# First norm of chunk 0 moved into the convolution, turned blocks given to engines by name, one weight load on another queue, and three changed orders in the main loop

## The chip, the cores and the metric

One core of a Trainium2 chip runs one launch of one program. The core has five engines that run their own instruction streams in order and meet at semaphores: TensorE (PE, matrix products; PEld is its weight load), VectorE (DVE), ScalarE (ACT), GpSimd (POOL) and SyncE (SP). The last two, and ACT now and then, also issue DMA transfers. The metric is the time of one execution on the device in microseconds (us). Lower is better.

## What is computed

Two kinds of layer alternate, and the kernel computes the output and, through the derivative of the whole, the gradients of eight inputs:

```python
def _A_ref(q, k, v, shift_k, ssm_k, ssm_D):
    k_shift = sum over 4 taps of k shifted in time * shift_k
    kv = k_shift * v
    y = irfft(rfft(kv, 2S) * rfft(ssm_k, 2S))[:S]      # a long convolution
    return q * (y + kv * ssm_D)

def _B_ref(x, w1, w2):
    return silu(x @ w1) @ w2

x = A_q
x = x + _A_ref(_layernorm(x), A_k, A_v, A_shift_k, A_ssm_k, A_ssm_D)
x = x + _B_ref(_layernorm(x), B_w1, B_w2)
x = x + _A_ref(_layernorm(x), ...)       # the same weights again
x = x + _B_ref(_layernorm(x), ...)
```

The sequence has S = 2048 places, the model D = 448 channels, the hidden layer F = 1792; all arrays are bf16. The convolution y does not depend on x, so it is computed once and used by both A layers. The results are x and the gradients by q, k, v, shift_k, ssm_k, ssm_D, w1 and w2.

## The kernel before

The work has three stages. `_ssm_prefix` (0 to about 103 us) computes the convolution with Fourier matrices on PE. `Main.run` (about 103 to 512 us) takes the sequence in four chunks of 512 places (four tiles of 128) through both layers, forward and back. `_ssm_suffix` and `Jobs` (to the end) carry the gradient through the convolution and sum the gradients of w1 and w2.

**Order.** The order of PE's instructions in the main stage is the order in which the program records them. A scheduler orders the other engines, mostly by the order of recording as operands become ready, and each engine then keeps its list in order: an instruction that waits holds up all that stand behind it. Tiles of one tag share a fixed number of buffers, and an allocation waits until the buffer's last user is done. A POOL transfer waits, besides its operands, until the eighth POOL transfer before it has landed.

**The prefix around the change.** Two passes over the channel halves h = 0, 1 each run four rounds. A round makes the four-tap convolution of four tiles (`conv`, PE L392), copies it (ACT `ks`, L395), stores it (POOL, L397), multiplies it by v (DVE L398), and does the first Fourier step of the round before (`stage1_kv`, PE L408, copies to A1kv). In the pass h = 0 a round also turns two blocks of the filter's transform (`turn`, PE L370, 16 transposes of 128x128 a block, one copy of 128x2048). In the pass h = 1 a round also does the second Fourier step of the filter (PE L217, copies to ZK). The first layer norm of chunk 0 (`ln0`, a generator over `_ln_steps`) takes one step in each round of h = 1: the statistics of one tile (DVE L271, L274). Behind the rounds it runs to its end: `ln_ve` (DVE L277), the power -1/2 on POOL (L279, `rstd`), `ln_nmr` (DVE L282), four `na` (ACT L285) and a store of them (POOL L290). Then come the half swaps: 14 transfers on POOL (L253, L254) that write the filter's spectrum with real and imaginary halves exchanged, and which must land before the products can use them; four stores of the spectrum (L445); w1, loaded by three transfers on SP (L447 to L449) and in part cleared by POOL (L450). Then seven blocks of A1kv are turned (L370 again), with copies given to ACT or DVE by a running estimate of both loads (`bal.pick`). After that come 14 chunks: a Fourier step (PE L217), a copy (ACT or DVE, again `bal.pick`), the product with the spectrum and its swapped copy (`pab`, DVE L471), 16 small matmuls (`ps_v`, PE L235, L236) two chunks later, and a copy of those (ACT).

**The main loop around the change.** `H` makes the hidden layer (PE L513 into `ps_h`; ACT takes Silu to `aT`, L673, and copies the input of Silu to `dT`, L678; a few copies are DVE's, L676). `O` multiplies by w2 (PE L695 into `ps_o`; DVE adds the result to X, L699, which frees one of two PSUM buffers of the tag "po"). `G` and `N` are the way back: N multiplies by w1 transposed (PE L741 into `ps_n`, the same two buffers; ACT copies it, L745, and DVE runs a chain of small operations for each tile, L915 to L920, L748 to L755). `T` transposes a normed chunk (PE L580, ACT copy L581). `fwd0b(c)` is the second norm of chunk c: statistics (L271, L274), `ln_ve` (L277), POOL's power (L279), four `n` (L287). `fwd0(c)` is the first norm and the gate (L287, L621, L622). `weave` takes a pattern of letters, one step of a generator for each letter. One step of O or N is half a tile, seven matmuls of 128x448; two steps of N are a tile. One step of H is one pair of hidden blocks, seven in a chunk. In iteration c the order is O of chunk c in layer 2, the product of ghT with dT (DVE L866), N with H of chunk c+1 in layer 1, O, then G, and N with H of chunk c+1 in layer 2.

Of the kernel before, what the change touches and what calls it, by code (L numbers as in the profile page):

```python
# [17 lines left out]
P = 128  # L18
# [90 lines left out]
def _copy(nc, eng, out, in_):  # L109
    if eng is nc.scalar:  # L110
        return nc.scalar.copy(out, in_)
    return eng.tensor_copy(out, in_)
# [148 lines left out]
def _ln_steps(k, pool, c, src, si, n_g, groups=((0, 4),), pin=False, eng=None, behind=None, store=()):  # L261
    nc = k.nc
    for lo, hi in groups:
        n = hi - lo
        st = pool.tile([P, 4, 6], FP32, name="ln_st", tag="ln_st", bufs=1)
        mv = pool.tile([P, 4, 2], FP32, name="ln_mv", tag="ln_mv", bufs=2)
        for tl in range(lo, hi):
            with ExitStack() as es:
                if behind:
                    es.enter_context(k.tc.issue_after(behind[tl].ins))  # L270
                i = nc.vector.bn_stats(out=st[:, tl, :], in_=src(tl))  # L271
            if pin:
                k.tc.keep_in_program_order(i)
            nc.vector.bn_aggr(out=mv[:, tl, :], in_=st[:, tl, :])  # L274
            yield
        ve = pool.tile([P, 4], FP32, name="ln_ve", tag="ln_ve", bufs=2)
        nc.vector.tensor_scalar(out=ve[:, 0:n], in0=mv[:, lo:hi, 1], scalar1=EPS, scalar2=None, op0=ALU.add)  # L277
        r = k.rstd[si][:, 4 * c:4 * c + 4]
        k.ln_pow = nc.gpsimd.tensor_tensor(out=r[:, lo:hi], in0=ve[:, 0:n], in1=k.mhalf[:, 0:n], op=ALU.pow)  # L279
        if eng is nc.scalar:  # L280
            nmr = pool.tile([P, 4], FP32, name="ln_nmr", tag="ln_nmr", bufs=1)
            nc.vector.scalar_tensor_tensor(out=nmr[:, lo:hi], in0=mv[:, lo:hi, 0], scalar=-1.0, in1=r[:, lo:hi], op0=ALU.mult, op1=ALU.mult)  # L282
        for tl in range(lo, hi):
            if eng is nc.scalar:
                nc.scalar.activation(n_g[:, tl, :], src(tl), ACT.Identity, bias=nmr[:, tl:tl + 1], scale=r[:, tl:tl + 1])  # L285
            else:
                k.ln_last = nc.vector.tensor_scalar(out=n_g[:, tl, :], in0=src(tl), scalar1=mv[:, tl, 0:1], scalar2=r[:, tl:tl + 1], op0=ALU.subtract, op1=ALU.mult)  # L287
    if si != 2 and store is not None:
        lo, hi = store or (groups[0][0], groups[-1][1])
        nc.gpsimd.dma_start(out=_pm(k.N_d[si][:])[:, 4 * c + lo:4 * c + hi, :], in_=n_g[:, lo:hi, :])  # L290
# [7 lines left out]
def _ssm_prefix(k):  # L298
    nc, tc = k.nc, k.tc
    bal = k.bal  # L300
    k_pm = _pm(k.A_k[0])
    v_pm = _pm(k.A_v[0])
    with ExitStack() as es:
# [20 lines left out]
        Zkv = A1K[:].rearrange("p a c n s -> p a (c n s)")  # L324
# [24 lines left out]
        for dc in range(ND):  # L349
            kview = ksb[dc].rearrange("p (n1 n2) -> p n2 n1", n2=16)  # L350
            pt = psum.tile([P, 2, 1024], BF16, name="ps_kt", **a_)
# [12 lines left out]
        bal.reset()  # L364
        A1Kf = A1K[:].rearrange("p a c n s -> p (a c n s)").rearrange("p (a b) -> p a b", b=P)

        def turn(src, dst, g):
            pt = psum.tile([P, 16, P], BF16, name="ps_tr", **a_)
            for i in range(16):
                nc.tensor.transpose(pt[:, i, :], src[:, 16 * g + i, :], k.ident[:])  # L370
            _copy(nc, bal.pick(2048, dve_ns=0.53), dst[:, 16 * g:16 * g + 16, :], pt[:])

        for jq in range(4):
            pt = psum.tile([DC, ND, 4, P], BF16, name="ps_kT", **a_)
# [47 lines left out]
        ln0 = _ln_steps(k, work, 0, lambda tl: k.x0c0[:, tl, :], 0, k.na0, pin=True, eng=nc.scalar)  # L422

        prev = None
        for h in range(2):
            for i, jq in enumerate((1, 2, 3, 0)):
                kvt = conv(h, jq)
                if prev:
                    stage1_kv(*prev)
                prev = (h, jq, kvt)  # L430
                if h == 0:
                    for g in (2 * i, 2 * i + 1):
                        if g < 7:
                            turn(A1Kf, Z, g)
                else:
                    _fft_stage2(k, Z, psum, cons_ka, range((0, 4, 8, 11)[i], (4, 8, 11, 14)[i]))
                    next(ln0, None)
        for _ in ln0:
            pass
        for i in range(7):  # L440
            _swap_halves_dma(k, KB, Ka, 2048 * i, 2048 * (i + 1), nc.gpsimd)
        stage1_kv(*prev)
# [1 line left out]
        for i in range(7):  # L444
            nc.gpsimd.dma_start(out=k.SPEC_d["K"][:, 2048 * i:2048 * (i + 1)], in_=Ka[:, 2048 * i:2048 * (i + 1)])  # L445
        k.w1sb = k.wk.tile([P, ND, F], BF16, name="w1sb", tag="WB")
        nc.sync.dma_start(out=k.w1sb[:, 0:3, :], in_=k.B_w1[0:384].rearrange("(c p) f -> p c f", p=P))  # L447
        nc.sync.dma_start(out=k.w1sb[64:128, 3, :], in_=k.B_w1[384:448, :])
        nc.sync.dma_start(out=k.w1sb[0:64, 3, 2 * P:], in_=k.B_w1[320:384, 2 * P:])  # L449
        nc.gpsimd.memset(k.w1sb[0:64, 3, 0:2 * P], 0.0)  # L450


# [2 lines left out]

        A1f = A1kv[:].rearrange("p a c n s -> p a (c n s)")
        for g in range(7):
            turn(A1f, Zkv, g)
        hold = []

        def cons_prod(ci, ps):
# [76 lines left out]
class Main:  # L538
# [245 lines left out]
    def run(self, es):  # L784
# [5 lines left out]
        def weave(pattern, **gens):  # L790
            for ch in pattern:
                next(gens[ch], None)
            for g in gens.values():
                if g is not jg:
                    for _ in g:
                        pass
# [6 lines left out]
        r = []  # L803
# [28 lines left out]
        r = []  # L832
# [4 lines left out]
        for c in range(4):  # L837

            aT2, dT2 = r
            self.slope(dT2)  # L840
            if c < 3:
                self.fwd0(c + 1)
            nT = self.nT() if c < 3 else None
            o = self.O(c, 1, aT2)
            steps("OOOO", O=o)
            if c in (1, 2):
                self.fwd0b(c + 1)
            if c == 0:
                weave("O" * 4, O=o)
                self.fwd0b(1)  # L850
            else:
                if c == 1:
                    gh2, g = gh21, g21
                else:
                    gh2 = []
                    g = self.G(gT, gh2)
                if c == 1:
                    weave("OGGOGGOTOT", O=o, G=g, T=self.T(self.n0[c + 1][1], nT))
                elif c < 3:
                    weave("OGOGGOGGGGTOT", O=o, G=g, T=self.T(self.n0[c + 1][1], nT))  # L860
                else:
                    jobs.start()
                    weave("OGOGGOGGGGO", O=o, G=g)
            for lo, hi in ((0, 4), (4, 7), (7, 8), (8, 12), (12, 13), (13, 14)):
                g = gh2[lo // 7][:, lo % 7:lo % 7 + hi - lo, :]
                nc.vector.tensor_tensor(out=g, in0=self.dpart(dT2, lo, hi), in1=g, op=ALU.mult)  # L866
            if c < 3:
                for hh in range(2):
                    self.store(("g", 1), gh2[hh], c, hh)
            gbc = gb  # L870
            n = self.N(c, 1, gh2, lambda tl: gbc[:, tl, :], self.n1[1], self.n1[0])
            G2 = self.X[:, 4 * c:4 * c + 4, :]
            gT = self.nT()
            gh1, dT0 = [], dT1
            tg = self.T(G2, gT)
            if c < 3:
                r = []
                if c == 0:
                    weave("NTNTNHNNHHNNHHNHH", N=n, T=self.T(self.n0[1][1], nT), H=self.H(c + 1, 0, nT, r, (10, 11)))
                else:  # L880
                    weave("NHNNHHNNHHNNHHN", N=n, H=self.H(c + 1, 0, nT, r))
                gb = gb_load(c + 1)
                aT, dT1 = r
                weave("OOOOOOTOTO", O=self.O(c + 1, 0, aT), T=tg)
                self.fwd1(c + 1, [self.chain] * 4)
                g = self.G(gT, gh1, dT0)
                if c:
                    gT = self.nT()
                    self.load_gT(c + 1, gT)
                    weave("G" * 7, G=g)  # L890
                else:
                    weave("G" * 7, G=g)
                self.slope(dT1, self.last_copy)
            else:
                weave("NJNJNJNJNJNJNJN", N=n, J=jg)
                for hh in range(2):
                    self.store(("g", 1), gh2[hh], c, hh)
                weave("J" * 11 + "TJJTJJJJ", T=tg, J=jg)
                weave("GGGJJGGJJGGJJ", G=self.G(gT, gh1, dT0, (1, 3, 5)), J=jg)
            for hh in range(2):  # L900
                self.store(("g", 0), gh1[hh], c, hh)
            n = self.N(c, 0, gh1, lambda tl: self.X[:, 4 * c + tl, :], self.n0[c][1], self.n0[c][0])
            if c < 3:
                r = []
                nT = self.nT()
                weave("NNTNTNHNNHHNNHHHH", N=n, T=self.T(self.n1[1], nT), H=self.H(c + 1, 1, nT, r, (10, 11)))
            else:
                weave("NJNNJNNJNNJN", N=n, J=jg)
        jobs.pool = None
# [473 lines left out]
```

## Time and profile before

| what | us |
|---|---|
| median of three runs | 716.89 (713.9 to 718.23) |
| the profiled execution | 716.31 |
| its span in the trace | 714.5 |
| PE busy in the span | 689.3 |
| DVE busy | 486.2 |
| ACT busy | 444.2 |
| POOL busy | 123.3 |

The span runs from the first to the last instruction in the trace; the time has 1.8 us more. A timeline row says when an instruction or a run of equal ones starts, how long it took, which engine, line and operation it is, the tiles (written <- read), their shapes, how many, and in brackets the idle time of that engine just before and what ended it. A row of waits gives the total, the number of times and the longest. Matmuls overlap, so a busy PE is a PE with work in its pipeline.

### The profile page before, as it was taken

The page shows a single profiled execution, that of the slowest core. Times are in us where ns is not written, and L with a number is a line of the kernel's source. Part 1 is how long each engine was busy: PE and PEld are TensorE (multiplying, and loading weights), DVE is VectorE, ACT ScalarE, POOL GpSimd, SP SyncE. Part 2 cuts the span into 40 slices and gives each one's busy share as a digit, 9 for nine tenths or more (in the row PEclk, how much of TensorE's full clock was granted, in tenths as well). Part 3 has the DMA queues.
Part 4 walks back from the last instruction along what each step waited for, and adds up shares of the span by engine and source line. Part 5 has one row for each costly group of instructions (what it writes and reads, how often), then busy time and mean ns, then how long its engine had stood idle before and what let it go on. Part 6 is the DMA issues. An engine that isn't in the chain of part 4 may idle for free.

```text
span 714.5 us, 12786 instructions
## 1 busy us (share of the span) xinstructions
PE 689.3 (96%) x5008; PEld 380.9 (53%) x5008; DVE 486.2 (68%) x1106; ACT 444.2 (62%) x582; POOL 123.3 (17%) x208
## 2 busy tenths in 40 slices
PE   6997899999999999999999999999999999999998
PEld 4886654434444444444444444544566666656655
DVE  4788776758887747877279723934258769869790
ACT  3878877686777868778677685132755555545200
POOL 1034420111011100111001100001212223353130
PEclk9999899999999999999999999999999999999999
DMA  9949998659969999499975999089999897879962
GB/s 303 305 146 234 342 287 255 168 139 270 236 146 235 215 240 242 116 243 231 224 179 133 233 229 365 3 187 249 309 413 357 291 343 245 266 274 377 354 181 95
DMA packets 196237, 172.59 MB, mean 242 GB/s; under 512 B 143090, under 2 KB 174194, under 8 KB 195024
## 3 DMA queue, kind: packets, MB, share of 16 engines
q1 hardware_dynamic: 181280, 115.30, 61.3%
q0 software_dynamic: 13344, 52.54, 20.9%
q10 hardware_dynamic: 1552, 3.94, 1.5%
q8 instruction: 39, 0.64, 0.4%
q14 instruction: 22, 0.18, 0.1%
HBM read 73.25 MB, written 60.10 MB: 187 GB/s over the span
## 4 chain that ended last, share of the span: by engine, by line
PE 62%; issue 8%; DVE 5%; ACT 4%; DMA 3%; POOL 2%; POOLq 0%; DVEq 0%; ACTq 0%
PE ps_d L995 12%; PE ps_n L741 12%; PE ps_h L513 11%; PE ps_g L513 10%; PE ps_o L695 7%; PE ps_d L1030 3%; ACT dT L688 2%; DMA ksf<-KS_d 1%; PE ps_t L580 1%; PE ps_gK L1305 1%; PE ps_tr L1211 1%; POOL rstd L279 1%; PE ps_d L1065 1%; PE ps_s L206 1%; DVE n L287 1%
## 5 line engine op out<-in xcount | busy, mean ns | idle before, releaser
L995 PEld LDWEIGHTS <-dstat 128*128 128x128 bf16 x768 | 72.5, 98 | 61.1
L513 PE MATMUL ps_h<-nT,w1sb 128*128 128x512 bf16 (+1 forms) x448 | 97.4, 380 | 2.6 <-ACT dT L678 1.9
L741 PE MATMUL ps_n<-w1T,ghT 128*128 128x448 bf16 x448 | 92.5, 353 | 0.8 <-DVE ghT L866 0.8
L695 PE MATMUL ps_o<-w2sb,aT 128*128 128x448 bf16 x448 | 88.5, 352 | 0.0
L513 PE MATMUL ps_g<-nT,w2T 128*128 128x512 bf16 (+1 forms) x392 | 82.9, 380 | 0.1
L723 ACT CAST ghT<-ps_g 128x512 bf16<-128x512 f32 (+1 forms) x74 | 54.1, 760 | 41.5 <-PE ps_g L513 41.2
L673 ACT ACTIVATE aT<-ps_h 128x512 bf16<-128x512 f32 (+1 forms) x82 | 60.0, 759 | 29.2 <-PE ps_h L513 27.6
L513 PEld LDWEIGHTS <-w1sb 128*128 128x128 bf16 (+1 forms) x448 | 35.5, 97 | 59.7 <-issue 25.4
L741 PEld LDWEIGHTS <-ghT 128*128 128x128 bf16 x448 | 43.2, 98 | 42.3 <-DVE ghT L866 1.7
L695 PEld LDWEIGHTS <-aT 128*128 128x128 bf16 x448 | 43.5, 98 | 40.1
L513 PEld LDWEIGHTS <-w2T 128*128 128x128 bf16 (+1 forms) x448 | 35.4, 97 | 55.1 <-issue 20.8
L915 DVE SCALAR_TENSOR_TENSOR lb_v<-lb_u,n 128x448 bf16<-128x448 bf16 x48 | 30.0, 624 | 46.8 <-ACT lb_u L745 46.3
L279 POOL TENSOR_TENSOR rstd<-ln_ve,mhalf 128x2 f32<-128x2 f32 (+2 forms) x27 | 23.0, 851 | 198.8 <-DVE ln_ve L277 198.8
L688 ACT ACTIVATE dT<-dT 128x1024 bf16<-128x1024 bf16 (+1 forms) x64 | 55.0, 940 | 0.1
L995 PE MATMUL ps_d<-n1m,dstat 128*128 128x448 bf16 x224 | 48.6, 352 | 0.0
L995 PE MATMUL ps_d<-n3m,dstat 128*128 128x448 bf16 x224 | 48.6, 352 | 0.0
L678 ACT CAST dT<-ps_h 128x1024 bf16<-128x1024 f32 (+1 forms) x50 | 42.8, 872 | 0.0
L745 ACT ACTIVATE lb_u<-ps_n,rstd 128x448 bf16<-128x448 f32 x32 | 20.7, 647 | 34.5 <-PE ps_n L741 26.3
L995 PE MATMUL ps_d<-X,dstat 128*128 128x448 bf16 x160 | 34.2, 353 | 0.0
L995 PE MATMUL ps_d<-go,dstat 128*128 128x448 bf16 x160 | 33.7, 353 | 0.0
L581 ACT COPY nT<-ps_t 128x1024 bf16<-128x1024 bf16 x20 | 20.2, 1008 | 18.7 <-PE ps_t L580 18.7
L866 DVE TENSOR_TENSOR ghT<-dT,ghT 128x512 bf16<-128x512 bf16 (+2 forms) x24 | 18.1, 778 | 19.2 <-ACT ghT L723 17.0
(217 smaller groups left out, 1245.1 us busy)
## 6 DMA issues: line engine op xcount, KB each, us to landing
dstat<-g_d SPq DMA_DIRECT2D x28, 512.0 KB, 5.6
dstat<-a_d SPq DMA_DIRECT2D x23, 512.0 KB, 7.1
a_d<-turned SPq DMA_DIRECT2D x16, 512.0 KB, 4.1
g_d<-turned SPq DMA_DIRECT2D x16, 512.0 KB, 3.9
a_d<-turned SPq DMA_DIRECT2D x16, 384.0 KB, 3.3
g_d<-turned SPq DMA_DIRECT2D x16, 384.0 KB, 3.3
N_d<-n POOLq DMA_DIRECT2D x10, 448.0 KB, 4.6
spec_K<-ZK POOLq DMA_DIRECT2D x7, 512.0 KB, 7.7
```

Source lines behind the costliest of these rows:

```text
L279: k.ln_pow = nc.gpsimd.tensor_tensor(out=r[:, lo:hi], in0=ve[:, 0:n], in1=k.mhalf[:, 0:n], op=ALU.pow)
L513: nc.tensor.matmul(ps(u, u + 1)[:, 0, :], lhsT=wT[h, b, ft * P:(ft + 1) * P], rhs=rhs[h, b, :], start=start, stop=stop)
L673: self.last_silu = nc.scalar.activation(aT[hh][:, o:o + hi - lo, :], ps(lo, hi), ACT.Silu)
L678: nc.scalar.copy(self.dpart(dT, 2 * fp + lo, 2 * fp + hi), ps(lo, hi))
L688: self.nc.scalar.activation(d[:, o:o + n, :], d[:, o:o + n, :], ACT.Derivative_silu)
L695: nc.tensor.matmul(po[:, :D], lhsT=aT[ft // 7][:, ft % 7, tl * P:(tl + 1) * P], rhs=self.w2sb[:, ft, :], start=(ft == 0), stop=(ft == NF - 1))
L723: nc.scalar.copy(g, ps(lo, hi))
L741: nc.tensor.matmul(pn[:, :D], lhsT=gh[ft // 7][:, ft % 7, tl * P:(tl + 1) * P], rhs=self.w1T[:, ft, :], start=(ft == 0), stop=(ft == NF - 1))
L745: nc.scalar.activation(u0[:], pn[:, :D], ACT.Identity, scale=k.rstd[2 * L + 1][:, t:t + 1], accum_out=cp[:, tl, 0:1])
L915: nc.vector.scalar_tensor_tensor(out=v[:], in0=u0, scalar=-1.0 / D, in1=n_t, op0=ALU.mult, op1=ALU.mult, accum_out=cp[:, 1:2])
L995: self.nc.tensor.matmul(ps[:, :D], lhsT=st[:, t, :], rhs=mov[:, t, :], start=(first and t == 0), stop=(last and t == NT - 1))
L1030: nc.tensor.matmul(ps[ft][:, :D], lhsT=get(t), rhs=mov[:, t, :], start=ft not in seen, stop=(last[ft] == i and t == hi - 1))
```

## The change

- `_ln_steps` yields once more, between POOL's power and what uses it. `ln0` takes its four steps of statistics in the rounds of h = 0 and its last two in the first two rounds of h = 1; the loop that ran it out is gone.
- The turned blocks of A1kv are copied by ACT (blocks 0, 3 and 6) and by DVE (1, 2, 4 and 5) by name, and the estimate of loads is reset behind them.
- w1 is loaded by POOL, behind the half swaps and the four stores, instead of SP.
- In iteration 0 the second norm of chunk 1 (`fwd0b(1)`) is recorded behind the product of ghT with dT instead of ahead of it.
- Iteration 0: the weave of N, T and H goes from NTNTNHNNHHNNHHNHH to NNTNTNHNNHHNNHHHH.
- Iterations 0, 1 and 2: the weave of N, T and H of layer 2 goes from NNTNTNHNNHHNNHHHH to NNTNTNHNHNHHNHHNH.

```diff
@@ _ln_steps
         k.ln_pow = nc.gpsimd.tensor_tensor(out=r[:, lo:hi], in0=ve[:, 0:n], in1=k.mhalf[:, 0:n], op=ALU.pow)
+        yield
         if eng is nc.scalar:
@@ _ssm_prefix
-        def turn(src, dst, g):
+        def turn(src, dst, g, eng=None):
...
-            _copy(nc, bal.pick(2048, dve_ns=0.53), dst[:, 16 * g:16 * g + 16, :], pt[:])
+            _copy(nc, eng or bal.pick(2048, dve_ns=0.53), dst[:, 16 * g:16 * g + 16, :], pt[:])
...
                         if g < 7:
                             turn(A1Kf, Z, g)
+                    next(ln0)
                 else:
                     _fft_stage2(k, Z, psum, cons_ka, range((0, 4, 8, 11)[i], (4, 8, 11, 14)[i]))
                     next(ln0, None)
-        for _ in ln0:
-            pass
...
-        nc.sync.dma_start(out=k.w1sb[:, 0:3, :], in_=k.B_w1[0:384].rearrange("(c p) f -> p c f", p=P))
-        nc.sync.dma_start(out=k.w1sb[64:128, 3, :], in_=k.B_w1[384:448, :])
-        nc.sync.dma_start(out=k.w1sb[0:64, 3, 2 * P:], in_=k.B_w1[320:384, 2 * P:])
+        nc.gpsimd.dma_start(out=k.w1sb[:, 0:3, :], in_=k.B_w1[0:384].rearrange("(c p) f -> p c f", p=P))
+        nc.gpsimd.dma_start(out=k.w1sb[64:128, 3, :], in_=k.B_w1[384:448, :])
+        nc.gpsimd.dma_start(out=k.w1sb[0:64, 3, 2 * P:], in_=k.B_w1[320:384, 2 * P:])
...
         for g in range(7):
-            turn(A1f, Zkv, g)
+            turn(A1f, Zkv, g, nc.vector if g % 3 else nc.scalar)
+        bal.reset()
@@ Main.run
             if c == 0:
                 weave("O" * 4, O=o)
-                self.fwd0b(1)
             else:
...
                 nc.vector.tensor_tensor(out=g, in0=self.dpart(dT2, lo, hi), in1=g, op=ALU.mult)
+            if c == 0:
+                self.fwd0b(1)
...
                 if c == 0:
-                    weave("NTNTNHNNHHNNHHNHH", N=n, T=self.T(self.n0[1][1], nT), H=self.H(c + 1, 0, nT, r, (10, 11)))
+                    weave("NNTNTNHNNHHNNHHHH", N=n, T=self.T(self.n0[1][1], nT), H=self.H(c + 1, 0, nT, r, (10, 11)))
...
-                weave("NNTNTNHNNHHNNHHHH", N=n, T=self.T(self.n1[1], nT), H=self.H(c + 1, 1, nT, r, (10, 11)))
+                weave("NNTNTNHNHNHHNHHNH", N=n, T=self.T(self.n1[1], nT), H=self.H(c + 1, 1, nT, r, (10, 11)))
```

## The prediction

> **What bounds the kernel now.** I read the page's busy times first, then PE's waits, then timelines of the three places that the diff touches.
>
> ```profile
> PE 689.3 (96%) x5008; PEld 380.9 (53%) x5008; DVE 486.2 (68%) x1106; ACT 444.2 (62%) x582; POOL 123.3 (17%) x208
> ...
> PE ps_v L235 <- DVE pab L471: 7.4, 5, 3.6
> ...
> PE ps_h L513 <- ACT dT L678: 1.9, 4, 0.5
> ```
>
> PE is at work for 689.3 of 714.5 us, so a change can only remove PE's waits or make new ones. The largest by cause, 7.4 us, lies in the convolution; in the main loop the waits are 0.5 us apiece. From 457 us to the end PE waits 0.8 us in all: whatever is lost or won ahead of that reaches the end in full.
>
> In the convolution (DVE, then ACT, then POOL):
>
> ```profile
> 62.74 0.16 DVE L277 TENSOR_SCALAR ln_ve<-ln_mv 128x4 f32<-128x4 f32 x1
> ...
> 64.07 0.16 DVE L282 SCALAR_TENSOR_TENSOR ln_nmr<-ln_mv,rstd 128x4 f32<-128x4 f32 x1
> ...
> 72.98 2.43 DVE L471 TENSOR_TENSOR pab<-A1K,ZK 128x2048 bf16<-128x2048 bf16 x2 [1.66 <-DMA ZK<-ZK]
> 77.12 1.23 DVE L112 CAST A1K<-ps_s 128x1024 bf16<-128x1024 f32 x1 [1.70 <-PE ps_s L217]
> ...
> 65.32 2.72 ACT L285 ACTIVATE na<-x0c,ln_nmr,rstd 128x448 bf16<-128x448 bf16 x4
> ...
> 62.99 1.04 POOL L279 TENSOR_TENSOR rstd<-ln_ve,mhalf 128x4 f32<-128x4 f32 x1 [3.25 <-DVE ln_ve L277]
> ```
>
> The norm's tail sits in the worst place: ACT spends 2.72 us on `na` while the copies that the first product needs stand behind it, and POOL holds the half swaps for `ln_ve` and `na` (3.25 and 2.74 us). PE waits 3.65 us for the first product, until 70.25. Windows of half a microsecond show the price:
>
> ```profile
> 69.00:69.50 0.50, 0.00 (x0) 0.52 1.07 223
> ...
> 75.50:76.00 0.50, 0.50 (x9) 0.65 1.15 301
> ```
>
> The third column is the granted clock: half from 69.0 to 75.7, some 6.7 us, and the 128x128 matmuls of that stretch stand 0.107 us apart instead of 0.056.
>
> In the main loop, the place of `fwd0b(1)` and that of the second weave:
>
> ```profile
> 158.21 10.76 PE L695 MATMUL ps_o<-w2sb,aT 128*128 128x448 bf16 x56
> ...
> 172.00 1.56 PE L741 MATMUL ps_n<-w1T,ghT 128*128 128x448 bf16 x6 [0.77 <-DVE ghT L866]
> ...
> 167.45 1.67 POOL L279 TENSOR_TENSOR rstd<-ln_ve,mhalf 128x4 f32<-128x4 f32 x1 [0.59 <-DVE ln_ve L277]
> ...
> 237.03 1.31 DVE L287 TENSOR_SCALAR n<-x0c,ln_mv,rstd 128x448 bf16<-128x448 bf16 x4
> ```
>
> **The change, part by part**, against the profiled execution's 716.31 us (0.6 below the median of 716.89).
>
> *Norm into the convolution.* Three tiles' statistics (L271 with L274, 0.7 us each) go into DVE's idle of 0.76 to 1.05 us a round of h = 0 and cost nothing there; in h = 1, where DVE has no gap from 45 to 60, 2.8 us leave. The fourth round pays: as built, DVE's order has `ln_ve` and `ln_nmr` next to each other, ahead of the A1kv copy that began at 43.60. Between the two lay 1.33 us above, filled by a copy; now DVE stands still for POOL's power. DVE's idle of 0.86 us there covers the statistics only, so the copy, and the stores, multiplies and copies behind it, start 1.2 us later. ACT takes two `na` (1.36 us) in each of two rounds with 0.90 us of idle, and falls 0.5 to 0.9 us behind. Behind the rounds ACT is rid of 2.72 us but has three turned blocks (1.87 each, it had two). Walking ACT from 60.1 plus 0.5 to 0.9 through blocks 0, 3 and 6, the last of which PE has ready at about 65.7, brings the first product to 68.1 to 70.3, where it was 68.97.
>
> *Swaps and w1.* POOL no longer stops for the norm, and w1's 1.76 MB leave the rings while the swaps run (DMA share 1.01 from 58 to 70). I take the 1.66 us for ZK to go. w1 lands in the 90s at the latest by its place behind the last store of the spectrum (issued at 77.96) and the row's 9 to 12 us; its reader starts at 109.22. Behind it in POOL's queue stand the clearing of w2T (read at 102.66) and seven stores; the last store waits for data until 92.80 anyway. Taken at nothing; bound below.
>
> *Sum of the prefix.* From the first product to the last DVE idles 1.66 + 1.70 + 0.46 + 1.16 = 4.98 us. The gain cannot exceed that; the loss is bounded by the 1.3 us of a late first product, its waits kept. PE's idle ahead of the product stays near 3 to 4 us, so I expect the half clock again, which explains the 1.70. What remains is a delay of about 1 us against the wait for ZK, part of which only exchanges places with PE's slow stretch: 0, between -5.0 and +1.3.
>
> *`fwd0b(1)` and the first weave.* As built, DVE alternates the four statistics with X additions and ghT products, and the last statistics stand behind the third addition, the norm's end behind the fourth, which needs the end of O. From 163.15: four statistics (0.54), three small L274 (0.09), ghT pieces (1.11 + 0.86 + 0.33 + 1.11 + 0.33 + 0.33) and three additions (0.52) make 8.06, to 171.2. Then L274 and `ln_ve` to 171.45; on POOL the output store stands ahead of the power (0.54, to 171.85); power 1.04 to 1.67; four `n` 1.32: 174.2 to 174.85. ghT is done at 170.1, in time for the second N step. PE would want T at 168.81 + 2 x 1.32 = 171.5 and finish it at 171.9; it finishes at 174.4 to 175.0, so 2.5 to 3.1 us are lost. Before, the second T starts at 173.40, where back-to-back work gives 171.89: 1.5 us. Net +1.0 to +1.6, taken +1.3. The weave now ends in HHHH, as the second weave did before, whose third H waited 0.47 for ACT: +0.5.
>
> *The second weave*, three times. HHHH (0.47) becomes two pairs HH, each behind an N whose copy (0.83 with its reading) delays ACT: up to 0.5 each, taken 0.4: +0.3 a time. More costly: the last half tile of N moves behind six of the seven H. It ended at 233.27, 7.3 us ahead of O (240.60); now one H of six full matmuls (1.3 us) is left, so it ends at 239.3. DVE's chain starts 1.0 later and takes 2.75 (234.28 to 237.03 before), and behind it stand, in order, `n` (1.24), gate and X (1.07 each), and only then O's first addition (0.52): 246.95. O's third tile needs that PSUM buffer at 240.60 + 2 x 2.65 = 245.9. A new wait of 1.1 us, in iterations 0 and 1 (behind the third weave `fwd0` is not called). Bounds: 0, if the scheduler's order leaves the addition free, to 2. Sum: 0.9 + 2.2 = 3.1.
>
> Total: 0 + 1.3 + 0.5 + 3.1 = +4.9, so **721.2 us**.
>
> **Rivals.** *A second half clock.* The wait for T at 171.5 is a new PE gap: about 1.4 us without work, then pairs of transposes held by one `n` each until 174.3. The row for it: a window with 1.0 us of PE work, 65.6 to 69.0, ended in half clock; one with 1.1 us idle (78.4 to 79.5) did not. 2.5 to 3.1 us fall between. A stretch of 3.4 to 6.7 us at half clock, with PE at work throughout, costs 1.7 to 3.4: 723.9 in the middle. The Trainium skill's "TensorE: Matmul & The Clock Gate", in its table "Why this matters for your kernels", tells to leave no PE gaps of more than about 3 us, and its Part 1 has the clock judged in free-running windows of 3.4 us. By that rule the phase decides, and the same kernel could fall either way from run to run. Its Part 4 says that transposes do not count as work; here 6.41 us of nothing but transposes (58.89 to 65.30) kept the clock at 1.00, and the trace decides.
>
> *Faster: the prefix pays.* If the first product comes at 68.1 and PE's gap ahead of it shrinks under the length that trips the clock (between 1.1 and 3.65 us by these rows), the stretch at half clock goes, with it the 1.70, and the swaps take the 1.66 away: up to 5.0 less. That meets +4.9, and where POOL's power takes 1.04 and the O addition slips ahead of the gate, 2.2 more are free: 714, below before. It decides at the first product: earlier than about 68.3, the clock may hold. Against it: the stall of 1.2 us and ACT's third block.
>
> *Stores behind w1.* If w1's 1.76 MB (5.3 us at 334 GB/s, the rate from 80 to 100) come on top of the queue, the last store of KV, issued at 92.80 and 8.3 on its way, lands at 106 instead of 101. The memory of ghT lies where the convolution's tiles were, and its first copy ran at 103.72: +2.5 and 723.7. Against it: the same bytes are moved in the same time as before, only in another order.
>
> *Nothing of it counts.* DVE's and ACT's slack hides the new waits: 716.3.
>
> **How the numbers follow.** Chances: forecast 0.46; second half clock 0.26; the prefix pays 0.15; stores 0.08; nothing 0.05. A measurement of this kernel tells about 1% (7.2 us) from no change: slower means above 724.1, faster below 709.7. Above 724.1 lie half or more of the half-clock case (0.15), half of the stores (0.04) and the tail of the forecast, where power and waits take their upper bounds (0.07): 0.26. Below 709.7 lies the end of the prefix case, without the waits of the second weave (0.05). The rest, 0.69, is within. The range reaches from the prefix case's middle with the forecast's waits partly there, 715.5, to the half clock of two windows on the forecast's upper bounds, 726.5, which leaves 0.1 below and 0.1 above.
>
> **What would show it.** Right: an idle PE of 1.5 us or more ahead of T (L580 before, 581 after) near 172 with DVE's `n` as releaser; a wait of PE `ps_o` for DVE's X addition of about 1 us near 246 and 337; DVE idle about 1.3 us for `rstd` near 44. The prefix term is right if `ps_y` starts within 1.5 us of 95.89, and wrong if it starts at 93 or earlier with the clock at 1.00 from 69 to 76. The half clock shows in PEclk near 172. I am wrong as a whole if PE's waits after 100 us sum to no more than before: then DVE's order, not its amount of work, was misread.

## The result and the profile after

Seven runs of the changed kernel have a median of 722.83 us (719.5 to 727.66), seven of the kernel before 714.83 (713.9 to 718.23). The ratio is 1.0102, with a 95% interval of 1.0065 to 1.014: slower, by 4.6 to 10.0 us. Six more runs beside other kernels gave 722.63 and 1.0101 (1.0077 to 1.0125); two of the six took 732.9 and 734.5 us at a mean clock of 0.988 and 0.991, and the ratio is that of the others. The profiled execution took 722.83 us, its span is 721.0.

PE's waits in the changed kernel, by what ended them (total, times, longest, in us):

```profile
PE ps_v L235 <- DVE pab L472: 5.6, 4, 2.8
...
PE ps_h L514 <- ACT dT L679: 3.3, 8, 0.5
PE ps_o L696 <- DVE X L700: 2.1, 2, 1.0
PE ps_t L581 <- DVE n L288: 2.1, 1, 2.1
...
PE ps_v L229 <- DVE pab L472: 1.3, 1, 1.3
...
PE ps_d L997 <- DMA dstat<-a_d: 1.0, 2, 0.7
PE ps_s L217 <- DVE A1kv L112: 1.0, 1, 1.0
```

Four causes are new or longer: PE's wait for DVE's A1kv in the convolution, for `n` ahead of T, for X ahead of O, and four more waits for ACT's `dT`. One cause is smaller: the two rows of waits for the products (L235, and L229 for the last chunk) make 6.9, where it was 7.4 in one row. The wait for `dstat` lies in the last stage, where the change edits nothing.

The table goes from landmark to landmark on PE: each number is the difference of two row starts in the timeline. Stretches left out differ by 0.03 us at most.

| stretch on PE | before | changed | difference |
|---|---|---|---|
| start to the first tap of the convolution | 26.19 | 25.00 | -1.19 |
| second pass to the first turned block | 15.49 | 16.89 | +1.40 |
| first turned block to the first product | 11.36 | 10.54 | -0.82 |
| first product to `ps_y` | 25.64 | 24.81 | -0.83 |
| first weave, N to O | 24.41 | 28.29 | +3.88 |
| second weave, N to O, iterations 0, 1, 2 | 23.88, 24.02, 24.01 | 24.17, 24.30, 24.32 | +0.88 |
| O and what follows to the next N, iterations 0, 1 | 18.17, 23.45 | 19.16, 24.58 | +2.12 |
| last stage, first `ps_d` to the end | 270.78 | 271.93 | +1.15 |

The differences sum to 6.6 us; the spans differ by 6.5. The first row is the arrival of the first load, at the start of every run, and no part of the change.

**The convolution.** DVE in the changed kernel, at the end of the norm:

```profile
42.33 0.17 DVE L277 TENSOR_SCALAR ln_ve<-ln_mv 128x4 f32<-128x4 f32 x1
43.73 0.16 DVE L283 SCALAR_TENSOR_TENSOR ln_nmr<-ln_mv,rstd 128x4 f32<-128x4 f32 x1 [1.23 <-POOL rstd L279]
43.81 1.08 DVE L112 CAST A1kv<-ps_s 128x896 bf16<-128x896 f32 x1
45.35 2.35 DVE L112 CAST ZK<-ps_s 128x1024 bf16<-128x1024 f32 x2
```

DVE stands still for 1.23 us with the copy of A1kv queued behind, and PE waits 0.95 for that copy at 44.95.

**Ahead of T.** PE, then DVE, then POOL, then windows around T (in the windows, the granted clock is the number behind POOL's):

```profile
167.34 2.81 PE L742 MATMUL ps_n<-w1T,ghT 128*128 128x448 bf16 x14
172.21 1.64 PE L581 MATMUL ps_t<-ident,n 128*128 128x128 bf16 x8 [2.06 <-DVE n L288]
173.64 2.80 PE L742 MATMUL ps_n<-w1T,ghT 128*128 128x448 bf16 x7
```

```profile
169.96 0.17 DVE L277 TENSOR_SCALAR ln_ve<-ln_mv 128x4 f32<-128x4 f32 x1
171.76 1.32 DVE L288 TENSOR_SCALAR n<-X,ln_mv,rstd 128x448 bf16<-128x448 bf16 x4 [1.63 <-POOL rstd L279]
```

```profile
170.12 0.54 POOL L702 DMA_DIRECT2D out_dram<-X  x1 [4.71 <-DVE ln_ve L277]
170.68 1.04 POOL L279 TENSOR_TENSOR rstd<-ln_ve,mhalf 128x4 f32<-128x4 f32 x1
```

```profile
172.00:172.50 0.50, 0.23 (x1) 0.10 (x1) 0.50 (x3) 0.00 (x0) 0.00 (x0) 1.00 1.17 433
...
173.00:173.50 0.50, 0.47 (x5) 0.38 (x5) 0.50 (x2) 0.00 (x0) 0.13 (x1) 0.50 1.21 246
...
176.50:177.00 0.50, 0.50 (x9) 0.41 (x7) 0.46 (x4) 0.08 (x1) 0.00 (x0) 1.00 0.79 293
```

PE idles from 170.15, T is then held by one `n` after the other, and from 172.9 to 176.3 the clock is half: seven matmuls of N take 2.80 us where 1.49 is usual.

**In the second weave and ahead of O**, in iteration 0 (iteration 1 shows the same 1.04 at 338.28):

```profile
235.20 0.39 PE L514 MATMUL ps_h<-nT,w1sb 64*128 64x512 bf16 x2 [0.40 <-ACT dT L679]
...
243.29 5.46 PE L696 MATMUL ps_o<-w2sb,aT 128*128 128x448 bf16 x28
249.79 1.48 PE L696 MATMUL ps_o<-w2sb,aT 128*128 128x448 bf16 x7 [1.04 <-DVE X L700]
```

DVE, first before the change and then in the changed kernel:

```profile
243.99 0.59 DVE L699 TENSOR_TENSOR X<-X,ps_o 128x448 bf16<-128x448 bf16 x1
```

```profile
245.76 1.31 DVE L288 TENSOR_SCALAR n<-x0c,ln_mv,rstd 128x448 bf16<-128x448 bf16 x4
...
249.12 1.15 DVE L700 TENSOR_TENSOR X<-X,ps_o 128x448 bf16<-128x448 bf16 x2
```

Between the two rows of the changed kernel lie the gate and X (L622, L623). O starts at 240.60 before and at 243.29 now: DVE's first addition of O's result began 3.39 us behind that start and begins 5.83 us behind it now.

### The profile page after: what moved, and what is told of

The parts are those of the page before. It is cut to its first block, busy times and chain, and to the rows that moved or that the text cites. A ratio compares the mean times of both kernels' runs of the same rounds, so it can differ in the third digit from the quotient of the medians.

```text
span 721.0 us, 12787 instructions
## 1 busy us (share of the span) xinstructions
PE 690.1 (96%) x5008; PEld 380.3 (53%) x5008; DVE 487.3 (68%) x1106; ACT 444.7 (62%) x582; POOL 124.2 (17%) x211
## 4 chain that ended last, share of the span: by engine, by line
PE 70%; DVE 5%; ACT 4%; issue 3%; DMA 2%; POOL 1%; POOLq 0%
PE ps_d L997 19%; PE ps_n L742 11%; PE ps_g L514 10%; PE ps_h L514 9%; PE ps_o L696 7%; PE ps_d L1032 3%; DMA dstat<-a_d 2%; PE ps_v L236 2%; PE ps_v L235 2%; PE ps_t L581 1%; ACT aT L674 1%; ACT dT L679 1%; PE ps_gK L1307 1%; DVE n L288 1%; PE ps_d L1067 1%
## 5 line engine op out<-in xcount | busy, mean ns | idle before, releaser
L742 PE MATMUL ps_n<-w1T,ghT 128*128 128x448 bf16 x448 | 94.3, 356 | 0.0
L677 DVE CAST dT<-ps_h 128x512 bf16<-128x512 f32 (+1 forms) x26 | 19.1, 768 | 27.9 <-ACT aT L674 27.8
```

Source lines behind the costliest of these rows:

```text
L742: nc.tensor.matmul(pn[:, :D], lhsT=gh[ft // 7][:, ft % 7, tl * P:(tl + 1) * P], rhs=self.w1T[:, ft, :], start=(ft == 0), stop=(ft == NF - 1))
```

## The experiments

### The second weave alone

```diff
# the kernel before
-weave("NNTNTNHNNHHNNHHHH", N=n, T=self.T(self.n1[1], nT), ...)
+weave("NNTNTNHNHNHHNHHNH", N=n, T=self.T(self.n1[1], nT), ...)
```

> The kernel before with the second weave's new pattern alone. Theory A (each new PE wait reaches the end in full): three times +0.3 in the weave (two HH pairs that each wait 0.40 for ACT's copy to dT, in place of one wait of 0.47) and twice about +1.05 at O's fifth half tile, which waits for DVE's addition to X: +3.0 us in all, and nothing elsewhere. Theory B (the waits are made good before the end, because PE has slack in the last stage): below +0.8. Theory C (the pattern also shifts transfers, and the waits of 0.96 us for dstat in the last stage come from it): +4.

Ratio 1.0038 (1.0016 to 1.006), so +1.1 to +4.3 us. The stretches are 24.17, 24.31 and 24.31 in the weaves and 19.16 and 24.58 behind, the changed kernel's to 0.01: +3.00. Theory A. The profiled run also has a last stage 5.9 us longer (276.70), through one wait for `dstat` of 3.1 us and two windows at half clock behind it. Up to that wait the `ps_d` rows of the stage start where those of before start, within 0.03 us, so PE's order there is no reason for it. The +3.00 of the weaves and of O accounts for the middle of the interval without C; but the interval holds C's +4 too, and this profile has a wait for `dstat` that the one of before has not, so C is not excluded.

### The norm of chunk 1 and the first weave alone

```diff
# the kernel before
                 weave("O" * 4, O=o)
-                self.fwd0b(1)
...
                 nc.vector.tensor_tensor(out=g, in0=self.dpart(dT2, lo, hi), in1=g, op=ALU.mult)
+            if c == 0:
+                self.fwd0b(1)
...
-weave("NTNTNHNNHHNNHHNHH", ...)
+weave("NNTNTNHNNHHNNHHHH", ...)
```

> The kernel before with the second norm of chunk 1 behind the ghT product and the first weave's new pattern, nothing else. Theory A (a wait for n, and a clock that falls behind the gap): PE waits about 2 us ahead of T, against 0.8 for ghT before, and HHHH waits 0.47: +1.8 us without a window at half clock, +3.5 to +4 with one, so between runs +1.8 and +4. Theory B (the wait alone counts, the slow rows behind T were slow through DVE's n): +1.8 to +2.4 in each run, and the clock at 1.00 from 172 to 178.

Ratio 1.0029 (0.9996 to 1.0062): -0.3 to +4.4 us, so the timed runs alone show no loss. In the profile PE waits 2.06 us for `n`, a window at half clock follows, and the weave takes 28.42 us: +4.0, theory A for a run with the window. In the last stage this run waits 9.2 us once for `dstat` (the kernel before has runs up to 725.9 us as well).

### The prefix alone

```diff
# the changed kernel with Main.run as before
```

> The kernel before with the three edits of the prefix alone. Theory A (DVE's stall of 1.2 us for POOL's power is paid by PE in the rounds, the gain behind the rounds gives it back): the convolution's inverse (ps_y) starts within 0.5 us of before once both are counted from the first of the rounds (69.70 us before); the time changes by -0.5 to 0 us. Theory B (the prefix carries the part of the loss that the waits do not explain): +1.5 us or more.

Ratio 1.0037 (1.0004 to 1.0071): +0.3 to +5.1 us. Rounds 16.89, first product 10.55, both as in the changed kernel: +0.59. No window at half clock came here, and the products took 23.83 instead of 25.64. Yet the profiled time is 716.36, what the kernel before took with two such windows: the last stage is 1.8 us longer (272.58). Theory A's exchange is there: 1.40 us lost in the rounds, 0.81 given back behind them. Its bounds were missed: counted from the first of the rounds `ps_y` starts 1.22 us earlier than before and not within 0.5, since the half clock is gone, and the timed runs, 2.3 us above before by their medians, lie nearer to theory B. In this profile what is over lies in the last stage, where runs scatter; for the other runs that is not shown.

### PE kept at work ahead of T

```diff
# the changed kernel
         pt = k.psum.tile([P, 2, 512], BF16, name="ps_t", tag="tr", bufs=1)
+        for i in range(self.pad):       # 32 in iteration 0, else 0
+            nc.tensor.transpose(pt[:, 0, (i % 4) * P:(i % 4 + 1) * P], k.ident[:], k.ident[:])
```

> The changed kernel with 32 transposes of the identity, 1.8 us of work at full clock, ahead of T in iteration 0; T overwrites what they write, and nothing is left out. T still waits for DVE's n until about 172.2. Theory A (the idle gap ahead of T brings the half clock behind it): the clock stays at 1.00 from 172 to 178, the seven matmuls behind T take 1.5 us instead of 2.8, and the first weave is 1.5 to 2.1 us shorter than in the changed kernel. Theory B (what is slow there is not the gap's doing, or transposes do not count as work): the half clock stays and the weave takes 28.3 us as before.

```profile
171.09 1.95 PE L581 MATMUL ps_t<-ident 128*128 128x128 bf16 x32
173.31 1.37 PE L586 MATMUL ps_t<-ident,n 128*128 128x128 bf16 x8 [0.27 <-DVE n L288]
174.52 1.49 PE L747 MATMUL ps_n<-w1T,ghT 128*128 128x448 bf16 x7
```

The clock stays at 1.00 through 178, N takes 1.49, and the weave 26.76 us: 1.53 less. That is what theory A gave. But the unpadded kernel does the same in some runs (see the changed kernel again, below), so this run shows the price of the window, 1.53, and not that the padding prevents it. The time is not lower: the median of four runs is 723.5, and the profiled one, 726.47, waits 2.9 us for `dstat`.

### The statistics early, n late

```diff
# the changed kernel
                 weave("O" * 4, O=o)
+                lb1 = _ln_steps(self.k, self.ch, 1, self.xs(1), 1, self.n0[1][1])
+                for _ in range(5):
+                    next(lb1)
...
             if c == 0:
-                self.fwd0b(1)
+                next(lb1, None)
```

> The changed kernel with the statistics and the power of chunk 1's second norm recorded where they were before the change, and only its four n behind the ghT product. Theory A (DVE's order makes the wait for T: in the changed kernel the statistics stand behind additions and ghT pieces, so the power comes at 170.7): DVE ends ghT at about 170.0 and n at 171.2, PE waits about 1.1 us ahead of T instead of 2.06 (0.6 to 1.5), no half clock follows, and the first weave takes 25.0 to 25.9 us instead of 28.29 (24.41 before). Theory B (POOL's store and power are late in any place): a wait near 2 us stays and the weave takes 26.5 or more.

The weave takes 24.89 us, 0.1 under the range of A. The power runs from 166.14, the `n` from 170.03, and what is left of PE's wait is a T that takes 1.38 us instead of 0.61. Beside the changed kernel without half clock (26.76, see the changed kernel again, below) that is 1.87 us less, so DVE's order made the wait ahead of T: theory A. The one run took 722.73 us; its profile has 4.3 us more in the last stage than before.

### ln_nmr held back

```diff
# the prefix edits alone
+            i = nc.vector.scalar_tensor_tensor(out=nmr[:, lo:hi], ...)
+            if pin:
+                k.tc.keep_in_program_order(i)
...
                 kvt = conv(h, jq)
+                if h:
+                    next(ln0, None)
```

> The prefix edits alone, with ln_nmr held in program order behind the next round's multiply, so that DVE does not wait for POOL's power; the four na then go to ACT in one round. Theory A (the stall of 1.23 us on DVE is what the rounds lost): from the first step of the second pass to the first turned block 15.5 to 15.8 us (15.49 before, 16.89 with the change), and from there to the first product 10.6 or up to 1 more, since ACT is late by na. Theory B (the round pays for na on ACT, not for the stall): 16.5 or more in the rounds.

DVE does not stop for the power any more, and the rounds still take 16.64, within theory B's bounds. ACT, then DVE:

```profile
49.80 2.73 ACT L288 ACTIVATE na<-x0c,ln_nmr,rstd 128x448 bf16<-128x448 bf16 x4
52.42 0.90 ACT L398 CAST ks<-ps_cv 128x896 bf16<-128x896 f32 x1
```

```profile
53.36 0.62 DVE L401 TENSOR_TENSOR ks<-ks,v_n 128x896 bf16<-128x896 bf16 x1 [0.65 <-ACT ks L398]
```

The four `na` fill ACT's 0.9 us of idle a round and 1.8 more; `ks` comes late, DVE waits for `ks`, PE for DVE (0.75). But this run puts all four `na` into one round, and the changed kernel has them two and two. From one start of `conv` to the next in the second pass, the changed kernel is longer than before by 1.06 us in the round of the stall and by 0.05 and 0.29 in the two rounds with `na`; this run is longer by nothing in the first and by 1.15 in the one that holds all four. So the stall made most of the changed kernel's 1.40, and `na` costs about as much only in one piece.

### PE kept at work ahead of the first product

```diff
# the kernel before
     pv = psum.tile([P, 8, P], FP32, name="ps_v", **k.pt["v"])
+    if ci == 0 and not conj:
+        for i in range(48):
+            nc.tensor.matmul(pv[:, i % 8, :], lhsT=k.ident[:], rhs=k.ident[:], start=True, stop=True)
```

> The kernel before with 48 matmuls of the identity, 2.7 us at full clock, in PE's idle ahead of the first product; the first product overwrites what they write, and nothing is left out. Theory A (the half clock from 69 to 76 follows from that gap): no window at half clock there, and 23.8 to 24.3 us from the first product to ps_y instead of 25.64. Theory B (the clock falls there for another reason): 24.7 or 25.6, as with one window or two.

The first product comes after the same 11.36 us, no half clock follows, and `ps_y` is 24.44 us behind it, not 25.64: theory A, 0.14 above its range. Two windows there are worth 1.2 us. It is one run, but of the 48 runs of the kernel before beside these experiments only one has a mean clock of 1.00. The one run took 714.01 us, beside 714.21 before.

### The turned blocks unnamed

```diff
# the prefix edits alone
-            turn(A1f, Zkv, g, nc.vector if g % 3 else nc.scalar)
-        bal.reset()
+            turn(A1f, Zkv, g)
```

> The prefix edits without the naming of engines for the turned blocks: two blocks on ACT and five on DVE, as before. From the first turned block to the first product, 11.36 us before and 10.55 with all prefix edits. Theory A (the gain of 0.81 is ACT's, which is rid of na, and the third block on ACT gives a part of it back): 9.8 to 10.5. Theory B (naming makes the gain): 11.0 to 11.4. The rounds ahead keep their 16.9 us in both.

9.21 us, below theory A's range: naming is not the gain, and the third block on ACT, which naming brings, takes 1.34 back. The 2.15 gained here (11.36 less 9.21) are not ACT's alone, though. ACT starts its first copy for the products 6.88 us behind the first turned block, 2.17 earlier than before (9.05); but this kernel also loads w1 by POOL, and the next pair of runs shows that ACT without `na` gives only 0.32 while w1 stays on SP. The products take 23.07, and `ps_y` is 3.3 us ahead of before, counted from the second pass. The gain did not last. SP's queue, then PE:

```profile
92.88 29.09 SPq L549 DMA_TRANSPOSE w1T<-in_B_w_dram  x1
...
135.88 1.23 SPq L766 DMA_TRANSPOSE nT<-in_grad_out_dram  x1
```

```profile
133.30 0.61 PE L780 MATMUL ps_t<-ident,n 128*128 128x128 bf16 x8
137.18 0.81 PE L513 MATMUL ps_g<-nT,w2T 128*128 128x512 bf16 x3 [3.27 <-issue]
138.34 2.14 PE L513 MATMUL ps_g<-nT,w2T 128*128 128x512 bf16 x5 [0.36 <-DMA nT<-in_grad_out_dram]
```

The transposing load of w1T held SP's queue for 29.1 us (10.5 in the changed kernel, 10.6 before), the transposed loads of grad_out stand behind it, and PE, which now comes earlier, waits for them and then runs 3.4 us at half clock: 4.1 us given back.

### The norm late, with w1 on SP and on POOL

```diff
# the kernel before
-ln0 = _ln_steps(k, work, 0, ..., pin=True, eng=nc.scalar)
+ln0 = _ln_steps(k, work, 0, ..., pin=True)          # four na on DVE, held in program order
...
                         if g < 7:
                             turn(A1Kf, Z, g)
+                    next(ln0)
                 else:
...
-                    next(ln0, None)
-        for _ in ln0:
-            pass
+                    if i == 0:
+                        next(ln0)
...
         _fft_stage2(k, Zkv, psum, cons_prod)
+        for _ in ln0:
+            pass
...
# the second kernel also loads w1 by POOL, as the changed kernel does
```

> The kernel before with the norm's four statistics in the rounds of h = 0, the power in the first round of h = 1, and its four na on DVE behind the last product (1.32 us, where DVE idles 1.16) instead of ACT; turned blocks unnamed, w1 on SP, main loop as before. Theory A (PE's wait for the first product is ACT's work on na, and the gap it leaves brings the half clock): rounds 15.5 us, turned block to first product 9.2 instead of 11.36, no half clock behind, first product to ps_y 23.1 to 23.8 instead of 25.64; 4 to 4.6 us less at ps_y. At the end the same 4 less (0.994 to 0.995), or, if the transposing loads of grad_out then come too late for PE near 134, as when the prefix ran with unnamed turns, 0 to 1 less. Theory B (as the forecast had it: the gain exchanges places with waits for the half swaps): ps_y at most 1 earlier.

> The same with w1 on POOL behind the half swaps. Theory A (w1's queue decides how long the transposing load of w1T takes, 10.5 to 12.1 us in the profiles with w1 on SP, 21.6 to 29.1 in four of six with w1 on POOL): w1T takes over 20 us here and under 13 with w1 on SP, and the loads of grad_out behind it make PE wait 3 to 4 us near 134. Theory B (chance): either length in either kernel.

With w1 on SP: 1.0004 (0.9983 to 1.0025), no gain: 2.3 us less at `ps_y`, 3.3 more in the last stage of its profile. Theory A gave 4 to 4.6 less at `ps_y` and theory B 1 at most, so neither holds. With w1 on POOL: **0.9969 (0.9944 to 0.9995)**, 712.37 us beside 715.7, faster than both kernels. Ten of its twelve runs have a mean granted clock of 0.999 or 1.00, one of the 23 runs of before beside them has: PE's gap ahead of the first product is 1.50 us here and 3.65 there. Rounds are 15.50 in both. The first product takes 11.04 with SP and 9.21 with POOL, `ps_y` 23.67 and 23.07. POOL's swaps with w1 on SP:

```profile
58.19 0.52 POOL L254 DMA_DIRECT2D ZK<-ZK  x1
63.66 0.52 POOL L253 DMA_DIRECT2D ZK<-ZK  x1 [4.96 <-issue]
65.81 0.52 POOL L254 DMA_DIRECT2D ZK<-ZK  x1 [1.64 <-DMA ZK<-ZK]
```

SP issues w1's three loads at 54.69 to 55.74, and POOL's next swap cannot go out for 5 us. The swap that POOL issued at 55.15 lands 10.4 us later, at 65.53, and with it ends DVE's wait ahead of the first product, which DVE starts at 65.61. The row of that wait names ACT, whose third copy ended at 65.57, but the first product needs only the first copy, done at 63.74; with w1 on POOL it starts right behind that copy. With POOL, w1 goes at 69.89, the same swap (57.57) lands after 4.2 us, and the longest wait between two swaps that follow is 1.14. So w1's move pays 2.4 us (1.83 and 0.60), once ACT is not late itself. In the kernel before, the two limits stood side by side: the swap landed at 68.83, and ACT's copy was done at 68.94. The profile names only the later one, ACT. Either relief alone leaves the other; w1's move alone was not run. On w1T theory A falls: 17.7 us with SP, 13.6 with POOL. Of the 4.7 us that the second kernel gains from the second pass to `ps_y` (15.49 + 11.36 + 25.64 less 15.50 + 9.21 + 23.07), the last stage gives back 2.8 in the profile.

### The changed kernel again

> The changed kernel once more, for the spread. Theory A (fixed waits and a clock that falls or not): rounds of h = 1 16.9, turned block to first product 10.55, second weaves 24.17, 24.30 and 24.32, O behind them 19.16 and 24.58 as in its first profile; the first weave 28.3 with a window at half clock and 26.4 to 26.8 without; runs 5.9 to 7.5 us above the kernel before. Theory B: these lengths vary from run to run, too.

```profile
166.91 2.81 PE L742 MATMUL ps_n<-w1T,ghT 128*128 128x448 bf16 x14
171.78 1.37 PE L581 MATMUL ps_t<-ident,n 128*128 128x128 bf16 x8 [2.06 <-DVE n L288]
172.99 1.49 PE L742 MATMUL ps_n<-w1T,ghT 128*128 128x448 bf16 x7
```

The same wait of 2.06 us, and no half clock. The weave takes 26.76 and the first product to `ps_y` 23.85, both without half clock; the other stretches from the second pass to the last stage are those of the first profile to 0.01, and the last stage is 1.3 longer (273.23). Theory A, with the last stage left out. Two of these six runs and two of the first seven have a mean granted clock of 1.00 over the whole span; the rest have windows at half clock. The four without take 719.5 to 722.2 us.

## Why the prediction was right

**The total.** Forecast +4.9 and 721.2 us, in a range of 715.5 to 726.5. The profiled executions differ by 6.5, the medians by 8.0; without any window in the first weave the fixed waits make 0.59 + 2.35 + 3.00 = 5.9. The mechanism of the two larger terms held. That the median lies within 1.6 us of the forecast is in part luck: the sum had no term for a window in the first weave (1.53, kept among the rivals) and none for the last stage (+1.15 in the profile), and it kept the two windows of the convolution, where one or none came (0.83 and 1.8 us less in the products).

**The second weave, 3.1.** Measured 3.00 in three profiles: the changed kernel's two and that of the pattern alone. Both halves are as reasoned: two waits of 0.40 for one of 0.47, and 1.04 at O's fifth half tile, because the last tile of N puts `n`, gate and X ahead of O's addition on DVE.

**The first weave, 1.3 + 0.5.** Measured 2.35 without half clock (26.76 less 24.41). The part at T was right: from N's start to the first H the changed order takes 9.17 us for four N steps and T, which is 7.84 without the fourth N (1.33), where before it took 6.36: +1.48, within the bounds 1.0 to 1.6. The part that was mis-sized is HHHH, at +0.5. The row's wait of 0.47 is not its whole price: in the changed kernel the pairs of H from 188.30 start 3.86 and 3.47 us apart where 3.23 is usual, so HHHH costs 0.87.

**The second half clock, chance 0.26.** It is real and it is not the forecast's opposite: the same kernel has it in one profile and not in another, and its price is 1.53 us (28.29 less 26.76), not 1.7 to 3.4. The Trainium skill's "TensorE: Matmul & The Clock Gate", Part 1, has the activity judged in free-running windows of about 3.4 us. The traces agree: half clock comes in stretches of 3.41, 6.83 and 10.24 us. Its rule of gaps over about 3 us, in "Why this matters for your kernels", does not tell the cases apart here: 2.06 and 2.84 us idle brought a window in some runs, 3.34 (w1 on SP) brought none. No gap of 1.5 us or less had one behind it in these profiles.

**The prefix, 0 between -5.0 and +1.3.** Right as a sum, +0.59 without the clock and -0.25 in the profile, where one window at half clock came instead of two; the timed runs of the prefix alone allow +0.3 to +5.1. DVE's stall was forecast at 1.33 and is 1.23; the first product on DVE at 68.1 to 70.3 and starts at 68.36 (69.55 with the 1.19 us by which this run's first load came earlier); `ps_y` within 1.5 of 95.89 and starts at 94.45, of which 1.19 was there at the first tap. ACT's lateness through `na`, forecast at 0.5 to 0.9, costs PE 0.34 of the rounds' 1.40; the stall's round has the other 1.06. That ACT's third block takes back a part of what ACT gains by losing `na` was right, with 1.34 of 2.17. What the forecast overlooked is the second limit ahead of the first product: it gave w1's move the later wait for ZK alone, and did not see that the first product, too, stood within 0.11 us of waiting for a half swap. The wait of 1.66 for ZK went, but one of 1.12 came at 75.37, which ends as a store behind the swaps lands. Without w1's move ACT's relief is worth 0.32. That the product's start decides on the clock, with 68.3 as the bound, was too sharp: with a gap of 2.84 and the product later than that, two of six profiles (the prefix alone, the changed kernel again) keep the clock and four do not.

**Stores behind w1, chance 0.08.** Not seen: 72.89 us from `ps_y` to N, 72.92 before.

**Small slips of the reading.** The half clock before the change lasts 6.83 us, to 75.85, and not to 75.7. Not all waits in the main loop were 0.5 us apiece: one is 1.48 (DVE's `n`, at 143.70) and one 0.77. The middle of 1.7 to 3.4 gives 723.8 and not 723.9. None of them changes a term.

**What stays open.** The last stage took 270.7 to 270.8 us in two profiles (the kernel before, and that kernel with PE kept at work) and 271.6 to 281.7 in the eleven others, with waits for `dstat` of 0 to 9.2 us. Two of the eleven have the prefix of before, so the stage scatters without the prefix edits; whether they raise its mean was not settled. The 2 us between the fixed waits (5.9) and the medians (8.0) are not accounted for run by run: the windows in the first weave and the last stage are where the profiles differ, and the windows that the convolution lost make it more.

## What to carry to other kernels

When PE is busy nearly all of the span (96% here), cost an edit by what then stands ahead of the released instruction in the other engine's queue: a norm moved "into idle time" brings its power, its multiplies and its statistics as a chain, and any link of it can stand ahead of a copy that PE wants. Move the chain in pieces: statistics and power early, and the multiplies late, on the engine that is idle there. Together with w1's move to POOL that was worth 0.3% of the whole time; with w1 left on SP it was worth nothing, and the prefix edits as built, with the chain whole and the turns named, cost 0.4%. With w1 on POOL and unnamed turns in both, the split chain reaches `ps_y` 1.4 us earlier than the whole one, counted from the second pass (47.78 and 49.17 us). Look for the second limit behind a wait: the profile names the one that ended last, and ahead of the first product another had ended 0.11 us before it. Compare kernels by stretches between landmarks; two profiles then agree to 0.01 us in all but the clock and the transfers, and the scatter of whole runs no longer hides 3 us.

## What the runs showed of the hardware

One transposing load of the same 1.6 MB held its queue for 10.5 to 29.1 us in thirteen profiles of nearly equal kernels, without a cause that these runs name; what stands behind it in the queue needs that slack.

A transfer can be slowed by loads on another queue: the same 256 KB half swap landed after 10.4 us with w1's three loads issued on SP in the same microsecond, and after 4.2 us with w1 behind the swaps on POOL (the two kernels with the norm late).
